# A two-layer attention and MLP kernel on one Trainium2 core: two weight loads moved from ScalarE's queue to GpSimd's, and the order of work settled anew

## The chip, the core and the metric

The kernel runs on one core of one Trainium2 chip. A core has engines that each follow their own list of instructions and wait for one another by semaphores: TensorE (PE; its weight loads are the row PEld), VectorE (DVE), ScalarE (ACT), GpSimd (POOL) and SyncE (SP). SP, ScalarE and GpSimd can issue transfers (DMAs). An engine takes its instructions in order: one that waits holds up all behind it. SBUF is the core's memory of 128 partitions; PSUM, eight banks of 128 x 512 float32, takes TensorE's results. The metric is the device time of one execution, in microseconds (us); less is better.

## The reference

x is 2048 tokens of 512 bfloat16 numbers. Two layers, with the same weights, each do

```python
x = x + A(layernorm(x));  x = x + B(layernorm(x))
# A, linear attention, 32 heads of 16:
q, k, v = split(x @ wqkv);  phi(t) = where(t > 0, t + 1, exp(t)) + 1e-6
kv = phi(k)^T v;  z = sum over tokens of phi(k)        # per head
A  = (phi(q) kv / (phi(q) z + 1e-6)) @ wo
# B: B = gelu(layernorm(x) @ w1 + b1) @ w2 + b2,  512 -> 1792 -> 512
```

## The kernel before

All lies in one function, `build_kernel`. It first makes a graph of operations (each with its engine, its inputs and outputs, and an estimated duration), and then puts them on the engines in an order that is written out: `CONF["ORDER"]` holds one list of names for each engine, and `CONF["WAY"]` says on which engine, or in which form, an operation is done that could be done on several. `Scheduler` walks the lists, gives buffers and PSUM banks in that order, and `assign_waits` turns dependencies into semaphore waits. `N_K`, `N_N` and the like cap how many PSUM banks a class of results may hold while the banks are given out. So the order on the chip is the lists' order, whatever the transfers do.

The tokens are 16 tiles of 128, in four chunks of four. The names used below end in layer and tile, or layer, chunk and part:

- `x0`, `x1`, `xc1`, `xc2`, `xc3`: the loads of x (tile 0, tiles 1 to 3, chunks 1 to 3); `wk`, `wq`, `wv`: the three thirds of wqkv; `wo`; `w1_0`, `w1_1`, `w2_0`, `w2_1`: the halves of w1 and w2, issued by GpSimd through `late` (line 641) after all tiles of layer 0 are turned. x1, xc1, xc2, wq, xc3, wv and wo are issued in this order by ScalarE (lines 613 to 629), x0 and wk by SP.
- `stats`, `aggr` (VectorE), `veps`, `pow` (GpSimd, layer 0's first on VectorE), `norm` (VectorE, or ScalarE with `nmr` on GpSimd ahead): the layer norm of a tile (lines 672 to 697).
- `TA`, `TB`: the turned (transposed) tile, mostly as a DMA of SP (line 707); in the first tiles as `PTA` on TensorE (line 720) with a copy `tcA` by ScalarE (line 730).
- `K`, `Q`: the projections (lines 771, 802, 789); `exp`, `relu` on ScalarE, `min`, `phi` on VectorE or GpSimd: their feature map (lines 741 to 758).
- `G`: products of normed x and phi(k) (line 867, layer 1 line 899), from which `KV` takes the attention state with wv (line 922); `Z`, `zs`, `zb`: the sums z, spread over a mask `bdmask` that GpSimd makes in two steps, `bdm0` and `bdm1` (lines 644 and 647); `M`: the state times wo (line 945).
- `D`, `ln`, `rec`, `pr` (lines 991 to 999): the denominators of a chunk; in other chunks `pz`, `red`, `den`, `rec`, `pr`, `TP` (lines 967 to 983).
- `WO` and `RA` (lines 1015, 1020): the attention's output added to x. `W1`, `gelu`, `W2`, `RB`, `b2` (lines 1047 to 1095, 1032): the MLP. `OD`: the output's store.
- `za`, `zhi`: layer 1's running sum of phi(k). `cpz`, `cpg`, `cpm`: copies out of PSUM. `warm`: ten matmuls on ones, while nothing has been loaded.

The matmul that waits at the start is `K0_0`; it needs `wk` and `tcA0_0`, ScalarE's eighth instruction after seven loads:

```python
"act": "x1 xc1 xc2 wq xc3 wv wo tcA0_0 reluk0_0 tcA0_1 expk0_0 tcA0_2 ..."
```

Of the kernel before, what the change touches and what calls it, by code (L numbers as in the profile page):

```python
# [10 lines left out]
P = 128  # L11
S = 2048
D = 512
# [253 lines left out]
def assign_waits(graph, order, sems, dma_sems):  # L267
# [10 lines left out]
    while len(done) < total:  # L278
        moved = False
        for e in ENGINES:  # L280
# [43 lines left out]
    N_HALF=1, N_K=2, N_Q=3, P_Z0=6.15, N_PB=1, N_PT=8, P_DEN=-50.43, P_A2=-55.11, P_W1=38.59, P_W2=10.23,  # L324
    P_K=55.79, P_G=131.85, P_Q=170.13, STEP=3.86, A1_Q=12.91, A1_STEP=0.5, N_H=4, N_N=3, GAP=28.61,
    ORDER={
        "pe":
            "warm PTA0_0 K0_0 PTA0_1 PTA0_2 K0_1 K0_2 PTA0_4 G0_0_0 PTA0_3 K0_4 K0_3 G0_1_0 Q0_0_0 Q0_0_1 PTA0_5 G0_2_0 K0_5 "
            "K0_7 G0_3_0 Z0_0 K0_6 G0_4_0 K0_8 Q0_1_2 K0_14 G0_5_0 K0_12 Z0_1 K0_15 G0_6_0 Q0_1_3 Q0_1_0 K0_13 G0_7_0 K0_10 "
            "K0_11 Q0_0_2 K0_9 G0_8_0 Q0_1_1 Z0_3 Z0_2 G0_9_0 Q0_0_3 G0_10_0 D0_0_1 G0_11_0 D0_0_0 G0_12_0 D0_0_2 G0_13_0 "  # L330
            "D0_0_3 G0_14_0 D0_1_0 ZR0 G0_15_0 G0_15_1 G0_15_2 Q0_2_0 KV0_0 G0_15_3 KV0_1 D0_1_1 KV0_2 D0_1_2 Q0_2_1 KV0_3 "
            "Q0_2_3 M0_0 M0_2 M0_3 Q0_2_2 M0_1 WO0_0_0 D0_1_3 Q0_3_1 WO0_0_1 WO0_1_0 WO0_0_2 Q0_3_0 WO0_0_3 WO0_3_0 Q0_3_2 "
            "WO0_2_0 WO0_4_0 Q0_3_3 WO0_5_0 WO0_7_0 WO0_6_0 W10_0_3_0 W10_0_4_0 W10_0_0_0 W10_0_9_0 W10_0_1_0 W10_0_7_0 "
            "W10_0_2_0 W10_0_5_0 W10_0_11_0 W10_0_8_0 W10_0_6_0 W10_0_10_0 W10_0_13_0 W20_0_0 W10_0_12_0 W10_0_6_1 W10_0_11_1 "
            "W10_0_0_1 W20_0_7 W10_0_4_1 W10_0_5_1 W10_0_7_1 W20_1_0 W10_0_1_1 W10_0_12_1 W10_0_8_1 W10_0_2_1 WO0_9_0 "
            "W10_0_3_1 W10_0_9_1 W20_1_7 W10_0_10_1 WO0_8_0 W10_1_0_0 W10_1_6_0 W10_1_1_0 W10_1_5_0 W10_1_2_0 W10_1_3_0 "
            "W10_1_4_0 W10_1_13_0 W10_1_12_0 W10_1_10_0 W10_1_7_0 W10_1_8_0 W10_1_11_0 WO0_11_0 WO0_10_0 W20_4_0 W10_1_9_0 "
            "W10_0_13_1 W20_5_0 W20_4_7 W20_5_7 K1_1 W20_7_0 W20_2_0 W20_7_7 W20_6_0 K1_0 W10_2_3_0 W20_6_7 WO0_14_0 "
            "W10_2_0_0 W20_2_7 WO0_13_0 W10_2_10_0 W10_2_1_0 W10_2_12_0 WO0_15_0 W10_2_8_0 WO0_12_0 W10_2_4_0 W10_2_6_0 "
            "W10_2_5_0 W10_2_7_0 W10_2_2_0 W10_2_9_0 W10_2_13_0 W10_2_11_0 W20_8_0 W20_10_0 W20_8_7 W20_10_7 W20_9_0 W20_11_0 "  # L340
            "W20_9_7 W20_3_0 W20_11_7 W10_3_7_0 W10_3_2_0 W10_3_1_0 W20_3_7 K1_2 W10_3_3_0 W10_3_5_0 W10_3_0_0 K1_5 W10_3_6_0 "
            "W10_3_9_0 W10_3_11_0 W10_3_10_0 W10_3_8_0 W10_3_13_0 K1_3 W10_3_12_0 W10_3_4_0 K1_6 K1_4 G1_0_3 G1_0_1 W20_12_0 "
            "G1_0_0 G1_0_2 W20_12_7 K1_7 K1_8 W20_13_0 W20_14_0 W20_13_7 K1_9 W20_14_7 W20_15_0 K1_10 W20_15_7 K1_11 G1_1_0 "
            "G1_1_3 G1_1_1 G1_1_2 Q1_1_1 Q1_1_0 Q1_1_2 K1_13 K1_12 Q1_1_3 Q1_0_0 K1_14 K1_15 Q1_0_2 Q1_0_1 ZH G1_2_1 Q1_0_3 "
            "Z1_3 G1_2_2 G1_3_1 D1_0_0 ZR1 G1_3_2 G1_2_0 G1_3_3 G1_3_0 D1_0_1 G1_2_3 D1_0_2 Q1_3_0 KV1_0 D1_0_3 Q1_2_0 KV1_1 "
            "Q1_3_1 KV1_2 Q1_3_2 KV1_3 Q1_3_3 M1_1 M1_3 M1_2 M1_0 Q1_2_1 WO1_0_0 WO1_1_0 WO1_0_1 Q1_2_2 WO1_0_2 WO1_0_3 "
            "WO1_2_0 WO1_3_0 WO1_4_0 WO1_5_0 PTB1_1 Q1_2_3 PTB1_0 WO1_6_0 W11_0_0_0 W11_0_8_0 W11_0_4_0 W11_0_3_0 W11_0_10_0 "
            "W11_0_12_0 W11_0_5_0 W11_0_2_0 W11_0_13_0 W11_0_1_0 W11_0_6_0 W11_0_9_0 W11_0_7_0 W11_0_11_0 W11_0_1_1 W11_0_2_1 "
            "W11_0_5_1 W11_0_6_1 W11_0_3_1 W11_0_4_1 W11_0_11_1 W11_0_9_1 W11_0_13_1 W11_0_8_1 W11_0_12_1 W11_0_10_1 "
            "W11_0_0_1 W11_0_7_1 WO1_7_0 W21_0_0 W21_1_0 W21_0_7 W21_3_0 W21_1_7 W21_2_0 W21_3_7 W21_2_7 WO1_13_0 W11_1_0_0 "  # L350
            "W11_1_1_0 W11_1_2_0 W11_1_6_0 W11_1_5_0 WO1_12_0 W11_1_10_0 W11_1_13_0 W11_1_3_0 WO1_15_0 W11_1_9_0 W11_1_7_0 "
            "WO1_14_0 W11_1_4_0 WO1_9_0 W11_1_12_0 W11_1_8_0 W21_4_0 W11_1_11_0 WO1_8_0 WO1_10_0 WO1_11_0 W21_5_0 W21_4_7 "
            "W21_6_0 W21_5_7 W21_7_0 W11_3_13_0 W11_3_2_0 W11_3_6_0 W11_3_4_0 W21_7_7 W11_3_0_0 W11_3_1_0 W21_6_7 W11_3_3_0 "
            "W11_3_5_0 W11_3_12_0 W11_2_4_0 W21_12_0 W11_3_10_0 W11_2_1_0 W11_2_5_0 W11_3_8_0 W11_3_7_0 W11_3_11_0 W11_2_12_0 "
            "W11_3_9_0 W11_2_7_0 W11_2_3_0 W11_2_2_0 W11_2_11_0 W11_2_10_0 W11_2_6_0 W11_2_9_0 W11_2_8_0 W11_2_0_0 W21_12_7 "
            "W11_2_13_0 W21_8_0 W21_9_0 W21_8_7 W21_9_7 W21_10_0 W21_13_0 W21_10_7 W21_11_0 W21_13_7 W21_14_0 W21_11_7 "
            "W21_14_7 W21_15_h0 W21_15_h1",
        "act":
            "x1 xc1 xc2 wq xc3 wv wo tcA0_0 reluk0_0 tcA0_1 expk0_0 tcA0_2 reluk0_1 expk0_1 tcA0_4 reluk0_2 tcA0_3 expk0_4 "
            "expk0_2 normA0_7 expk0_3 reluk0_3 expq0_0_0 reluq0_0_0 tcA0_5 expq0_0_1 normA0_8 reluq0_0_1 reluk0_5 normA0_14 "  # L360
            "expk0_5 reluk0_7 expk0_7 expk0_6 normA0_15 normA0_13 reluk0_8 reluk0_14 expk0_8 expk0_14 expk0_12 normA0_10 "
            "expk0_15 normA0_11 expq0_1_3 reluq0_1_3 expq0_1_2 reluk0_13 expq0_1_0 expk0_13 expk0_10 expk0_11 reluk0_11 "
            "expk0_9 expq0_0_2 reluq0_0_2 expq0_1_1 reluq0_1_1 expq0_0_3 ln0_0_1 rec0_0_1 ln0_0_0 rec0_0_0 ln0_0_2 rec0_0_2 "
            "ln0_0_3 rec0_0_3 cpz0 cpg0_2 ln0_1_0 expq0_2_0 rec0_1_0 ln0_1_1 expq0_2_1 rec0_1_1 ln0_1_2 cpm0_0 reluq0_2_1 "
            "cpm0_1 cpm0_3 rec0_1_2 ln0_1_3 rec0_1_3 expq0_2_2 expq0_3_1 reluq0_2_2 expq0_3_0 reluq0_3_0 expq0_2_3 reluq0_2_3 "
            "b1c reluq0_3_1 gelu0_0_4_0 gelu0_0_3_0 gelu0_0_9_0 gelu0_0_1_0 gelu0_0_7_0 gelu0_0_2_0 gelu0_0_0_0 gelu0_0_11_0 "
            "gelu0_0_5_0 gelu0_0_6_0 gelu0_0_8_0 gelu0_0_10_0 gelu0_0_13_0 gelu0_0_12_0 gelu0_0_6_1 gelu0_0_0_1 normB0_6 "
            "gelu0_0_11_1 gelu0_0_7_1 gelu0_0_5_1 gelu0_0_4_1 gelu0_0_1_1 gelu0_0_12_1 gelu0_0_8_1 gelu0_0_2_1 normB0_7 "
            "gelu0_0_9_1 gelu0_0_3_1 expq0_3_2 expq0_3_3 gelu0_0_10_1 gelu0_1_0_0 gelu0_1_6_0 gelu0_1_1_0 gelu0_1_2_0 "
            "gelu0_1_3_0 gelu0_1_4_0 gelu0_1_13_0 gelu0_1_12_0 reluq0_3_3 gelu0_1_10_0 normB0_9 gelu0_1_5_0 normB0_8 "  # L370
            "gelu0_1_7_0 gelu0_1_11_0 gelu0_1_8_0 gelu0_0_13_1 gelu0_1_9_0 normB0_11 expk1_1 gelu0_2_0_0 gelu0_2_3_0 reluk1_0 "
            "gelu0_2_10_0 expk1_0 gelu0_2_12_0 gelu0_2_8_0 gelu0_2_1_0 gelu0_2_4_0 gelu0_2_6_0 gelu0_2_5_0 gelu0_2_2_0 "
            "gelu0_2_7_0 gelu0_2_11_0 gelu0_2_9_0 gelu0_2_13_0 normA1_2 normA1_5 normA1_7 gelu0_3_2_0 gelu0_3_1_0 expk1_2 "
            "gelu0_3_7_0 normA1_6 gelu0_3_5_0 gelu0_3_0_0 gelu0_3_6_0 gelu0_3_9_0 gelu0_3_11_0 reluk1_2 gelu0_3_10_0 "
            "gelu0_3_3_0 gelu0_3_8_0 expk1_5 expk1_3 reluk1_3 gelu0_3_13_0 gelu0_3_4_0 normA1_9 reluk1_6 gelu0_3_12_0 expk1_6 "
            "normA1_11 expk1_4 normA1_10 expk1_7 expk1_8 reluk1_7 reluk1_8 expk1_9 reluk1_9 normA1_12 reluk1_10 expk1_10 "
            "expk1_11 reluk1_11 expq1_1_1 expq1_1_0 normA1_15 reluq1_1_2 expq1_1_2 reluk1_13 expk1_13 expk1_12 expq1_0_0 "
            "reluq1_0_0 expq1_1_3 expk1_14 reluk1_15 expk1_15 expq1_0_2 expq1_0_1 reluq1_1_3 reluq1_0_1 expq1_0_3 reluq1_0_2 "
            "ln1_0_0 cpz1 rec1_0_0 ln1_0_1 rec1_0_1 ln1_0_2 rec1_0_2 reluq1_3_0 expq1_3_0 ln1_0_3 rec1_0_3 reluq1_3_1 "
            "expq1_3_1 cpm1_1 cpm1_3 cpm1_2 expq1_2_0 expq1_3_2 reluq1_3_2 reluq1_2_1 reluq1_2_0 reluq1_3_3 expq1_3_3 "  # L380
            "normB1_1 expq1_2_1 tcB1_1 tcB1_0 gelu1_0_0_0 gelu1_0_4_0 gelu1_0_8_0 gelu1_0_10_0 gelu1_0_3_0 gelu1_0_12_0 "
# [132 lines left out]
def build_kernel(nc, A_x, A_wqkv, A_wo, B_x, B_w1, B_b1, B_w2, B_b2, out, conf=None, report=False):  # L514
# [5 lines left out]
    with ExitStack() as es:  # L520
# [9 lines left out]
        wqkv = SB("wqkv", [P, DT, 3 * D], BF16)  # L530
        wo = SB("wo", [P, DT, D], BF16)
# [108 lines left out]
        def late(name, key, dst, src, prio, kb, after):  # L640
            dma("pool", lambda e: e.dma_start(dst, src), [key], prio=prio, name=name, kb=kb, after=after)
# [635 lines left out]
```

## Time and profile before

| | |
|---|---|
| median of 4 runs | 332.0 us (331.5 to 332.44) |
| the profiled execution | 332.44 us, its span 330.7 us |
| granted TensorE clock, mean | 0.995 |
| TensorE busy | 320.1 us, 97% of the span |
| VectorE, ScalarE, GpSimd busy | 219.1, 199.1, 147.0 us |
| HBM read, written | 8.00 MB, 2.10 MB |

A row of the page's fifth part names line, engine, operation, output and inputs, then how many, busy time and mean length, then the idle time ahead of them and what ended it. "PE ps L771 <- ACT t L730" in a list of waits says that TensorE's instruction of line 771 waited for ScalarE's of line 730. Times within the execution count from the span's start. The granted clock is the share of full speed that TensorE was allowed. An engine name with a small q (ACTq) is its sequencer, as when it issues a DMA.

### The profile page before, as it was taken

The numbers are of one execution on the slowest core, as the hardware profiler recorded it, in microseconds if no ns is written. First come the engines' busy times: TensorE is split into PE (matmuls) and PEld (weight loads), VectorE is DVE, ScalarE is ACT, GpSimd is POOL, SyncE is SP. The second block draws the span as 40 slices with busy tenths as digits, with TensorE's granted clock in tenths as the row PEclk, the third lists the DMA queues.
The fourth block names the chain that finished last, engine by engine and source line by source line (L and its number), as shares of the span: only waits on it lengthen the run. The fifth ranks groups of instructions, "written<-read, shape, count | busy, mean of one in ns | idle before, by whom it ended". The sixth has DMA issues, their size and how long they took to land.

```text
span 330.7 us, 4722 instructions
## 1 busy us (share of the span) xinstructions
PE 320.1 (97%) x1688; PEld 158.7 (48%) x1718; DVE 219.1 (66%) x491; ACT 199.1 (60%) x333; POOL 147.0 (44%) x234
## 2 busy tenths in 40 slices
PE   5999999999999999999999999899999999999996
PEld 1444545486444444444444444448644444444444
DVE  6686677896967667454286889999969777400212
ACT  2697879676981457419992384869944532656200
POOL 3475616659534723336325615657455927000000
PEclk9799999999999999999999999999999999999999
DMA  7833535323112310233010200021143412300011
GB/s 267 257 64 65 135 124 164 92 48 65 33 32 50 63 32 3 48 65 62 2 41 7 52 16 0 2 48 34 33 97 76 84 38 59 80 0 2 16 57 54
DMA packets 49043, 20.37 MB, mean 62 GB/s; under 512 B 41916, under 2 KB 48316, under 8 KB 49020
## 3 DMA queue, kind: packets, MB, share of 16 engines
q1 hardware_dynamic: 44684, 12.86, 17.9%
q0 software_dynamic: 768, 3.67, 3.4%
q10 hardware_dynamic: 3568, 3.54, 3.3%
q8 instruction: 13, 0.21, 0.3%
q14 instruction: 10, 0.08, 0.1%
HBM read 8.00 MB, written 2.10 MB: 31 GB/s over the span
## 4 chain that ended last, share of the span: by engine, by line
PE 84%; DVE 7%; ACT 3%; ACTq 2%; DMA 1%; issue 1%; POOL 0%; DVEq 0%
PE ps L1047 29%; PE ps L1085 28%; PE ps L771 7%; PE ps L1015 7%; PE ps L789 3%; PE ps L867 3%; PE ps L802 2%; PE ps L899 2%; DMA t<-yb 1%; DVE xsb L1020 1%; PE ps L1072 1%; DVE rd L970 1%; ACT eb L741 1%; ACTq L628 1%; DVE rd L973 1%
## 5 line engine op out<-in xcount | busy, mean ns | idle before, releaser
L1053 ACT ACTIVATE gT<-ps,b1c 128x512 bf16<-128x512 f32 (+1 forms) x140 | 78.3, 601 | 65.6 <-PE ps L1047 64.9
L1047 PE MATMUL ps<-t,w 128*128 128x512 bf16 (+1 forms) x556 | 101.5, 336 | 0.3
L1085 PE MATMUL ps<-w,gT 128*128 128x512 bf16 x424 | 96.6, 379 | 0.5
L1047 PEld LDWEIGHTS ps<-t,w 128*128 128x128 bf16 x560 | 54.6, 98 | 44.1 <-ACT t L730 0.3
L1085 PEld LDWEIGHTS ps<-w,gT 128*128 128x128 bf16 x434 | 42.3, 98 | 50.3 <-ACT gT L1053 0.3
L741 ACT ACTIVATE eb<-ps 128x512 bf16<-128x512 f32 x64 | 37.3, 601 | 14.1 <-PE ps L771 7.3
L684 POOL TENSOR_TENSOR rstd<-veps,neghalf 128x1 f32<-128x1 f32 x64 | 37.9, 596 | 6.9 <-DVE veps L682 3.4
L1095 DVE TENSOR_TENSOR outb<-ps,xsb 128x512 bf16<-128x512 f32 x15 | 10.3, 689 | 39.8 <-PE ps L1085 37.8
L771 PE MATMUL ps<-wqkv,t 128*128 128x512 bf16 x125 | 32.3, 388 | 3.5 <-ACT t L730 2.9
L672 DVE BATCH_NORM_STATS2 stats<-xsb 128x6 f32<-128x512 f32 x48 | 32.1, 682 | 0.3
L1015 PE MATMUL ps<-gtb,t 128*128 128x512 bf16 x122 | 30.6, 379 | 0.9 <-DVE xsb L1020 0.3
L752 ACT ACTIVATE rb<-ps 128x512 bf16<-128x512 f32 x43 | 25.1, 606 | 6.1 <-PE ps L771 6.1
L1032 POOL TENSOR_TENSOR xsb<-xsb,b2b 128x512 f32<-128x512 f32 x17 | 20.2, 1195 | 6.1 <-DVE yb L697 6.0
L677 POOL TENSOR_SCALAR veps<-mv 128x1 f32<-128x1 f32 x32 | 8.0, 251 | 32.8 <-DVE mv L674 25.8
L1213 ACT ACT_TABLE_LOAD x17 | 21.8, 1283 | 0.3
L697 DVE TENSOR_SCALAR yb<-xsb,mv,rstd 128x512 bf16<-128x512 f32 x29 | 16.2, 563 | 8.5 <-POOL rstd L684 8.4
L692 ACT ACTIVATE yb<-xsb,nmr,rstd 128x512 bf16<-128x512 f32 x19 | 15.3, 810 | 10.2 <-POOL nmr L689 10.1
L1091 DVE TENSOR_TENSOR xsb<-ps,xsb 128x512 f32<-128x512 f32 x16 | 11.0, 689 | 15.3 <-PE ps L1085 15.2
L771 PEld LDWEIGHTS ps<-wqkv,t 128*128 128x128 bf16 x128 | 12.1, 99 | 18.6 <-ACT t L730 4.2
L789 PE MATMUL ps<-wqkv,t 128*128 128x512 bf16 x78 | 19.9, 379 | 0.1
L754 DVE TENSOR_SCALAR eb<-eb 128x512 bf16<-128x512 bf16 x43 | 14.1, 339 | 8.5 <-ACT eb L741 8.3
L1015 PEld LDWEIGHTS ps<-gtb,t 128*128 128x128 bf16 x128 | 12.2, 98 | 15.5 <-DVE xsb L1020 1.8
(89 smaller groups left out, 381.8 us busy)
## 6 DMA issues: line engine op xcount, KB each, us to landing
w<-in_B_w_dram POOLq DMA_DIRECT2D x4, 896.0 KB, 5.6
out_dram<-outb SPq DMA_DIRECT2D x15, 128.0 KB, 1.7
t<-in_A_x_dram ACTq DMA_DIRECT2D x3, 512.0 KB, 7.2
wqkv<-in_A_wqkv_dram ACTq DMA_DIRECT2D x2, 512.0 KB, 9.2
t<-yb SPq DMA_TRANSPOSE x56, 2.4
wqkv<-in_A_wqkv_dram SPq DMA_DIRECT2D x1, 512.0 KB, 5.2
wo<-in_A_wo_dram ACTq DMA_DIRECT2D x1, 512.0 KB, 9.3
t<-in_A_x_dram ACTq DMA_DIRECT2D x1, 384.0 KB, 3.3
```

The lines of the kernel that those rows point to most:

```text
L672: G.op("dve", lambda e: e.bn_stats(stats[:, s.slot, :], src()), 620, reads=src_keys, writes=[k + "s"], tiles=[s, *src_tiles], prio=prio, n ...
L684: G.op("pool", lambda e: e.tensor_tensor(rstd[:, s.slot:s.slot + 1], veps[:, s.slot:s.slot + 1], neghalf[:], op=ALU.pow), 570, reads=[k + ...
L741: G.op("act", lambda e: e.activation(eb[:, et.slot, :], bank(bt), ACT.Exp), 478, reads=[src_key], writes=[f"e{tag}"], tiles=[bt, et], prio ...
L752: G.op("act", lambda e: e.activation(rb[:, rt.slot, :], bank(bt), ACT.Relu), 478, reads=[src_key], writes=[f"r{tag}"], tiles=[bt, rt], pri ...
L771: ins = e.matmul(bank(b), lhsT=yTa(yT)[:, dt, k * P:(k + 1) * P], rhs=wqkv[:, dt, D:2 * D], start=(dt == 0), stop=(dt == DT - 1))
L789: ins = e.matmul(bank(b), lhsT=yTa(yT)[:, dt, k * P:(k + 1) * P], rhs=wqkv[:, dt, 0:D], start=(dt == 0), stop=(dt == DT - 1))
L1015: ins = e.matmul(bank(wb), lhsT=yTa(pq)[:, kt, k * P:(k + 1) * P], rhs=gtb[:, kt, :], start=(kt == 0), stop=(kt == DT - 1))
L1032: G.op("pool" if on_pool else "dve", lambda e: e.tensor_tensor(xsb[:, st, :], xsb[:, st, :], b2b[:], op=ALU.add), 1120 if on_pool else 600 ...
L1047: ins = e.matmul(bank(b, n), lhsT=w1[:, dt, ft * P:(ft + 1) * P], rhs=yTa(yT)[:, dt, k0 * P:k1 * P], start=(dt == 0), stop=(dt == DT - 1))
L1053: G.op("act", lambda e, ft=ft, b=b, k0=k0, k1=k1, n=n: e.activation(gT[:, g.slot, ft * 512 + k0 * P:ft * 512 + k1 * P], bank(b, n), ACT.Ge ...
L1085: ins = e.matmul(bank(b), lhsT=gT[:, g.slot, ft * 512 + k * P:ft * 512 + (k + 1) * P], rhs=w2[:, ft, :], start=(ft == 0), stop=(ft == FT - 1))
L1213: e.preload_act_table_set(sets[table])
```

## The change

wv and wo are no longer issued by ScalarE. GpSimd issues them through the same helper as w1 and w2, each allowed once tile 5 is turned (`tr` is that turn's last operation). In GpSimd's list wo stands behind nmrA0_13, and wv in a row of five loads.

```diff
-        dma("act", lambda e: e.dma_start(wqkv[:, :, 2 * D:3 * D], wsrc[:, :, 2 * D:3 * D]), ["wv"], prio=-94, name="wv", kb=512)
-        dma("act", lambda e: e.dma_start(wo[:], A_wo.rearrange("(dt p) c -> p dt c", p=P)), ["wo"], prio=-93, name="wo", kb=512)
...
+                if st == 5:
+                    late("wv", "wv", wqkv[:, :, 2 * D:3 * D], wsrc[:, :, 2 * D:3 * D], -88, 512, [tr])
+                    late("wo", "wo", wo[:], A_wo.rearrange("(dt p) c -> p dt c", p=P), -87, 512, [tr])
```

With it all five lists of `ORDER` are new, `N_K` goes from 2 to 4, `N_N` from 3 to 1, and 48 entries of `WAY` change. TensorE's list holds the same operations and differs by neighbours that change places, mostly by one to five us of work. The parts that the prediction speaks of:

```diff
 act:
-x1 xc1 xc2 wq xc3 wv wo tcA0_0 ...
+x1 xc1 wq xc3 xc2 tcA0_0 ...
-... reluq0_0_1 reluk0_5 normA0_14 expk0_5 ...
+... reluq0_0_1 normA0_14 reluk0_7 reluk0_5 ...
 pe:
-... K0_8 Q0_1_2 K0_14 G0_5_0 ...
+... K0_8 K0_14 Q0_1_2 G0_5_0 ...
 pool:
-... nmrA0_13 vepsA0_10 powA0_10 phiq0_0_1 nmrA0_10 ...
+... nmrA0_13 wo vepsA0_10 powA0_10 nmrA0_10 ...
-... powA0_9 phik0_14 bdm1 w2_1 phik0_11 w2_0 phiq0_0_2 pr0_0_3 w1_1 pr0_1_0 pr0_1_1 w1_0 ...
+... powA0_9 phik0_14 w2_0 wv w1_0 w1_1 eps6 w2_1 bdm1 pr0_0_3 pr0_1_0 pr0_1_1 ...
 WAY, from GpSimd to VectorE: b20_4 to b20_7, b20_11, b20_14, b20_15, pz0_3_0, pz0_3_3, pr0_3_2, pr0_3_3,
  phiq0_0_1, phiq0_0_2, phiq0_3_3, phik0_11, phik1_2, phik1_6, phiq1_1_2, za2, za4, za7, ...
 WAY, from VectorE to GpSimd: b20_8, b20_12, pr0_2_3, phiq0_3_0, za5, za11, ...
 WAY, other: normB0_8 from ScalarE to VectorE; phiq1_0_3 from the form with max to relu and add
```

## The prediction

> **What bounds the kernel now.** I read the page first: how full TensorE is, and the chain of work that ended last.
>
> ```profile
> span 330.7 us, 4722 instructions
> ...
> PE 320.1 (97%) x1688; PEld 158.7 (48%) x1718; DVE 219.1 (66%) x491; ACT 199.1 (60%) x333; POOL 147.0 (44%) x234
> ...
> PE 84%; DVE 7%; ACT 3%; ACTq 2%; DMA 1%; issue 1%; POOL 0%; DVEq 0%
> ```
>
> TensorE is the bound nearly everywhere, so only its waits can be won. Then the waits of TensorE, over the whole span (total, times, longest):
>
> ```profile
> PE ps L771 <- ACT t L730: 2.9, 2, 2.5
> ...
> PE ps L771 <- DMA t<-yb: 0.5, 1, 0.5
> PE ps L945 <- DVE kvb L941: 0.5, 1, 0.5
> PE ps L922 <- DVE gtb L912: 0.4, 1, 0.4
> ```
>
> The longest is the first K projection (line 771), which waits for ScalarE's copy of the first turned tile (line 730). Why that copy is late shows in the chain in order of time (start, length):
>
> ```profile
> 3.03 0.59 ACTq L613
> 3.65 2.24 ACTq L628
> 5.92 1.74 ACTq L629
> 7.70 0.61 ACT t L730
> 8.35 1.48 PE ps L771 x4
> ```
>
> ScalarE's sequencer issues seven loads before its first copy. The first five take 0.45 to 0.60 us each, the last two, wv and wo, 2.24 and 1.74: they wait for room, and the copy stands behind them. Last, the table by stretches (PE, PEld, DVE, ACT, POOL busy; granted clock; DMA share; GB/s), cut where the clock changes, and at the seam of the two layers:
>
> ```profile
> 5.40:8.82 3.42, 0.88 (x9) 0.47 (x8) 3.23 (x10) 0.60 (x1) 1.37 (x4) 1.00 1.09 362
> 8.82:12.23 3.41, 3.09 (x14) 1.47 (x13) 1.13 (x6) 2.06 (x4) 2.23 (x6) 0.50 1.11 350
> ...
> 197.00:222.00 25.00, 23.46 (x133) 10.57 (x135) 24.27 (x51) 17.16 (x32) 14.46 (x16) 1.00 0.08 16
> ```
>
> After the stretch in which TensorE mostly stood (0.88 us of 3.42), its clock was 0.50 for 3.41 us. At the seam VectorE is full (24.27 of 25) and TensorE waits.
>
> **The change part by part.** The profiled execution took 332.44 us, 1.74 more than its span; the median is 0.44 below it. I sum against 332.44 and take off 0.44 at the end.
>
> *wv and wo leave ScalarE.* The turn of tile 0 starts at 5.43 on TensorE. Later turns (14.41 and 18.95) have their copies 0.43 us after their start, at 14.84 and 19.38. So tcA0_0 can start at 5.86 instead of 7.70, and K0_0 0.65 behind it (7.70 to 8.35), at 6.51: **-1.84**. What is late next is the K weight itself: issued at 1.25, landing 5.2 us later, 6.45; so no more can be won at this place. All of the chain behind it is fed by K0_0 (reluk0_0, tcA0_1, K0_1, then ScalarE, busy 13.74 us in 12.23 to 27.20). normA0_1 ends at 7.08 and normA0_2 at 8.30, ahead of their turns. xc2 is now issued last, at 3.03; the slowest landing of such a load took 9.0, so it is there at 12.0, and statsA0_8, at 15.01 before, comes to 13.2. Nothing there eats the shift.
>
> *The slow clock.* K0_0 took 1.47 us where four matmuls take 1.03, and the next eight 2.49 where eight take 1.89: 1.04 us of this chain is slow clock. With K0_0 and two turns in it, the stretch before 8.82 would be about 1.9 us busy of 3.42 (0.39 + 1.03 + two turns of 0.25), between the row that was followed by 0.50 (0.88) and the one followed by 1.00 (3.09). Ends 0 and -1.04; I take **-0.4**, as 1.9 is a little nearer to 0.88. The Trainium skill (TensorE: Matmul & The Clock Gate, Part 1) has the clock halved after an idle window of 3.4 us; the row differs, as a window with a quarter of work was followed by half speed. By that rule the whole -1.04 would come, and the sum would be 0.6 lower.
>
> *K0_14 moves ahead of Q0_1_2.* K0_14 waited for the transpose of its tile:
>
> ```profile
> 22.86 4.14 DMA t<-yb
> 27.14 1.02 PE ps L771 x4
> ```
>
> The new order asks for it four matmuls (0.86) sooner, and turns ScalarE's reluk0_5 (0.49 from start to start) behind normA0_14: **+0.37**. Other transposes land in 2.4 at the median; if this one does, the 0.49 of idle time vanishes. Ends -0.5 and +0.9.
>
> *wo's issue on GpSimd* stands ahead of vepsA0_10. The four load issues there took 0.75 to 1.16, so about 0.95; phiq0_0_1 (1.15) leaves the same stretch for VectorE. nmrA0_10 was ready at 27.7 and its user normA0_10 began at 30.42: 2.7 us of cover. Its transfer now runs beside the transposes of tiles 12, 15 and 13. No row of before has a bulk load beside these; 512 KB at the 350 GB/s of the head are 1.5 us, and K0_15, at 30.13, had its transpose issued at 25.51, 2.2 us more than a median landing. Ends 0 and +0.5; I take 0.
>
> The Trainium skill (SBUF - State Buffer, SBUF: two separate sides) speaks against it: a GpSimd load's descriptors are written by that engine, which VectorE's two-port operations lock out, 620 ns becoming 3100 in its example. No row here shows this: the slowest issue took 1.16 with VectorE busy beside it. By the rule wo's issue would be some 2.2 longer, still under the 2.7 of cover, and the sum the same.
>
> *Five loads in a row on GpSimd.* In the new order w2_0, wv, w1_0, w1_1, w2_1 stand ahead of bdm1, the second half of the mask. Before, the mask came first, and issues stood apart:
>
> ```profile
> 33.46 1.25 POOL L758 TENSOR_TENSOR pkb<-eb,rb 128x512 bf16<-128x512 bf16 x1 [3.42 <-DVE eb L754]
> 34.66 0.91 POOL L647 TENSOR_SCALAR_AFFINE_SELECT bdmask<-bdmask 128x512 bf16<-128x512 bf16 x1
> 36.57 1.16 POOL L641 DMA_DIRECT2D w<-in_B_w_dram  x1 [0.99 <-DMA t<-yb]
> 38.47 1.15 POOL L758 TENSOR_TENSOR pkb<-eb,rb 128x512 bf16<-128x512 bf16 x1 [0.74 <-DVE eb L745]
> 39.57 0.95 POOL L641 DMA_DIRECT2D w<-in_B_w_dram  x1
> ```
>
> The first waits for the last transpose, 36.57 before, 34.7 with the shift. Five issues (1.16 + 0.95 + 0.76 + 0.75 + 0.95), eps6 (0.1) and bdm1 (0.91) end at 40.3. zb0, which reads the mask, would be due at 41.91 - 1.84 = 40.07: 0.2 late. It takes 0.69, and D0_0_1 came 1.28 us after its end: covered. Behind the loads wait also eps6 for ln0_0_1 (44.29) and pr0_0_3 (49.44), with room. wv, issued near 36, is read at 50.14 - 1.84 = 48.3, 12 us later, against 7.0 for the longest landing of such a load; wo is read later still. I take 0, the ends are in rival D. Whether GpSimd's queue takes four or five loads at once no row shows; before it had two in flight (issues at 36.57 and 39.57, landing after up to 7.0) and the second cost 0.95. That is rival D.
>
> *Work moved between engines.* In layer 0 five b2 additions (net), two pz, one pr and a norm go to VectorE: 5 x 0.85 + 2 x 0.76 + 0.86 + 0.54 = 7.2 us on top of 56.04 busy in 60 to 135, so 84% of the stretch. The list of TensorE's waits has none between 28 and 197, so this is covered. I take 0; ends 0 and +1.5.
>
> *The seam.* VectorE loses za11 (0.69) and 0.27 by another form of phiq1_0_3, and gains phiq1_1_2 (0.42): -0.5 on the full engine; ScalarE gains a relu (0.60) ahead of cpz1, GpSimd za11 ahead of zhi. I take 0; ends -1.0 and +1.0.
>
> *PSUM caps.* N_K 4 and N_N 1 set which banks the planner may hold; TensorE's order hardly moves and its work is the same (1718 weight loads in both lists). 0.
>
> Sum: 332.44 - 1.84 - 0.4 + 0.37 = 330.57; less 0.44, **330.1**.
>
> **The rivals.**
>
> A, the forecast: ScalarE's head wait is won, the rest cancels: 330.1 (329.2 to 331.3).
>
> B, more: the clock stays full (0.64 more than I took) and K0_14's wait vanishes (0.37 + 0.49): 328.6 (327.6 to 329.2). For it: TensorE has no other wait until the seam. Against: what held the 4.14 us landing the rows do not show, and it may come again.
>
> C, hidden: the shift is given back, 0.9 at K0_14 and 0.9 at the seam, where VectorE is full and starts no sooner than its inputs: 332.0 (331.4 to 332.6). For it: every later wait of TensorE is for the same few producers. Against: these producers hang on K0_0 too, through 170 us of saturated TensorE.
>
> D, slower: GpSimd's queue is full like ScalarE's. That one took 384 + 4 x 512 KB = 2.4 MB and then stopped; here the first three loads are 2.3 MB and the fourth makes it 3.2. If the fourth waits for the first (landing 6.2 after issue, 34.7 + 6.2 = 40.9) and the fifth for the second (some 43), bdm1 ends near 45, zb0 is 4.9 late, and D0_0_1 stands 4.9 - 1.3 = 3.6: 333.7. If only two are held, the third waits until 40.9, the fifth until about 47, and it is 338. It decides once the five issues take 1.1 us longer in all. Against it: issues of 0.75 to 1.16.
>
> E, slower too: at 84% VectorE, a norm in each of four chunks comes 0.7 late: 330.1 + 2.8 = 332.9. Against it: 12 us of VectorE's 75 are still idle there.
>
> That the change does not do what it says, the copy staying late, would need the turn at 5.43 to move; nothing ahead of it changes, so it has no share of its own.
>
> **How the numbers follow.** A 0.43, B 0.17, C 0.13, D 0.18, E 0.09. A difference under 0.2%, 0.66 us, can't be told from none here. Faster (A and B) 0.60, within it (C) 0.13, slower (D and E) 0.27. The range goes from 328.0 into D's first end, 334.0; left out are D's longer end and B's far one, under 0.2.
>
> **What would show it.** ScalarE's first copy at 5.9 and K0_0 at 6.5; ScalarE's five issues done at 3.6. The clock row after 8.8 shows 1.00 or 0.50. K0_14's wait. Five GpSimd issues of about 0.9 each and zb0 near 40. TensorE's waits between 28 and 197 still none. The forecast is wrong if one GpSimd issue takes over 2 us, if zb0 starts after 41.4, or if new waits of TensorE over 1.8 us in all appear.

## The result, and the profile after

The changed kernel takes **329.51 us** in the median of 51 runs (328.57 to 332.55). The kernel before, run again beside it, takes 331.15 us in the median of 77 (329.51 to 333.18); the 332.0 of the four runs above was a little high. The ratio is 0.9951, with a 95% interval of 0.9942 to 0.9961: faster by 1.6 us. The forecast had 330.1, 0.9943 of the time it was given.

The profiled execution took 328.61 us, its span 326.9. It differs from the profiled one of before by 3.8 us, more than the medians do: that one lay 1.3 above its kernel's median, this one 0.9 below its own. So the pair of traces shows where time can go, and only the runs show how often it does. Line numbers after the change are five or so lower: the K projection is line 766, the copy of a turned tile 725, a load by GpSimd 636.

From the page after:

```profile
span 326.9 us, 4727 instructions
...
PE 318.6 (97%) x1687; PEld 159.0 (49%) x1718; DVE 226.9 (69%) x512; ACT 195.4 (60%) x331; POOL 128.8 (39%) x215
...
PE 90%; DVE 6%; DMA 2%; issue 1%; ACT 0%; DVEq 0%
```

ScalarE's sequencer (ACTq) has left the chain. ScalarE's own instructions and issues from the start on show why (start, length):

```profile
0.82 0.45 ACTq L617 DMA_DIRECT2D t<-in_A_x_dram  x1
1.30 0.51 ACTq L610 DMA_DIRECT2D t<-in_A_x_dram  x1
1.83 0.53 ACTq L622 DMA_DIRECT2D wqkv<-in_A_wqkv_dram  x1
2.39 1.30 ACTq L610 DMA_DIRECT2D t<-in_A_x_dram  x2
6.00 0.60 ACT L725 ACTIVATE t<-ps 128x512 bf16<-128x512 bf16 x1 [3.92 <-PE ps L715]
```

Five issues end at 3.69, and the copy now waits for the turn on TensorE, not for the queue: 6.00 in place of 7.70. TensorE's waits after the change, behind the warm-up's 1.5 us, which is the same before and after:

```profile
PE ps L862 <- DVE pkb L742: 0.9, 1, 0.9
PE ps L766 <- ACT t L725: 0.8, 1, 0.8
PE ps L715 <- DVE yb L692: 0.6, 1, 0.6
```

The 2.9 us for the copies fell to 0.8, the 0.5 for a transpose at K0_14 is gone, and two waits are new, which the forecast did not have: 0.9 at G0_9_0 (line 862) for phik0_9, and 0.6 at the turn of tile 2 (line 715) for normA0_2. The same stretches as before, and the seam 2 us earlier (PE, PEld, DVE, ACT, POOL busy; clock; DMA share; GB/s):

```profile
5.40:8.82 3.42, 2.08 (x18) 1.24 (x16) 2.99 (x10) 1.63 (x4) 1.76 (x4) 1.00 1.08 366
8.82:12.23 3.41, 3.41 (x24) 1.65 (x22) 3.38 (x11) 3.10 (x7) 2.83 (x7) 1.00 0.79 247
...
195.00:220.00 25.00, 24.44 (x152) 11.91 (x153) 24.36 (x55) 19.09 (x35) 15.34 (x18) 1.00 0.08 16
```

The clock row stays at 1.00 here, and at the seam TensorE stands for 0.56 of 25 us where it stood for 1.54. How far each operation of TensorE starts ahead of its start in before gives the account of the pair: 1.63 us at K0_0; 2.5 at K0_4, with the clock; 3.16 behind K0_14; 2.3 behind G0_9_0, and so on through 195; 3.7 behind the seam. TensorE's work is the same, so these are its waits and its clock; the wait at tile 2 adds nothing to them, as K0_1 behind it waits until 8.87 for ScalarE's copy anyway.

### The profile page after: what moved, and what is told of

It is laid out like the page before. It is cut to its first block, busy times and chain, and to the rows that moved or that the text cites. A ratio compares the mean times of both kernels' runs of the same rounds, so it can differ in the third digit from the quotient of the medians.

```text
span 326.9 us, 4727 instructions
## 1 busy us (share of the span) xinstructions
PE 318.6 (97%) x1687; PEld 159.0 (49%) x1718; DVE 226.9 (69%) x512; ACT 195.4 (60%) x331; POOL 128.8 (39%) x215
## 3 DMA queue, kind: packets, MB, share of 16 engines
q10 hardware_dynamic: 2512, 2.49, 2.3%
## 4 chain that ended last, share of the span: by engine, by line
PE 90%; DVE 6%; DMA 2%; issue 1%; ACT 0%; DVEq 0%
PE ps L1042 29%; PE ps L1080 29%; PE ps L1010 8%; PE ps L766 8%; PE ps L784 4%; PE ps L862 4%; PE ps L797 3%; PE ps L894 2%; DMA t<-in_A_x_dram 2%; PE ps L1067 1%; DVE gtb L907 1%; DVE rd L965 1%; PE ps L986 1%; PE ps L940 1%; PE ps L843 0%
## 5 line engine op out<-in xcount | busy, mean ns | idle before, releaser
L679 POOL TENSOR_TENSOR rstd<-veps,neghalf 128x1 f32<-128x1 f32 x64 | 39.8, 626 | 7.7 <-DVE veps L677 3.8
L747 ACT ACTIVATE rb<-ps 128x512 bf16<-128x512 f32 x44 | 25.8, 603 | 10.4 <-DVE pkb L753 5.1
L766 PE MATMUL ps<-wqkv,t 128*128 128x512 bf16 x124 | 30.8, 379 | 1.0 <-ACT t L725 0.8
L784 PE MATMUL ps<-wqkv,t 128*128 128x512 bf16 x79 | 19.8, 379 | 0.1
L749 DVE TENSOR_SCALAR eb<-eb 128x512 bf16<-128x512 bf16 x44 | 12.8, 300 | 9.7 <-ACT eb L736 9.7
L687 ACT ACTIVATE yb<-xsb,nmr,rstd 128x512 bf16<-128x512 f32 x18 | 14.5, 812 | 6.6 <-POOL nmr L684 6.6
L1027 POOL TENSOR_TENSOR xsb<-xsb,b2b 128x512 f32<-128x512 f32 x12 | 15.9, 1340 | 4.9 <-ACT yb L687 4.2
```

The lines of the kernel that those rows point to most:

```text
L679: G.op("pool", lambda e: e.tensor_tensor(rstd[:, s.slot:s.slot + 1], veps[:, s.slot:s.slot + 1], neghalf[:], op=ALU.pow), 570, reads=[k + ...
L747: G.op("act", lambda e: e.activation(rb[:, rt.slot, :], bank(bt), ACT.Relu), 478, reads=[src_key], writes=[f"r{tag}"], tiles=[bt, rt], pri ...
L766: ins = e.matmul(bank(b), lhsT=yTa(yT)[:, dt, k * P:(k + 1) * P], rhs=wqkv[:, dt, D:2 * D], start=(dt == 0), stop=(dt == DT - 1))
L784: ins = e.matmul(bank(b), lhsT=yTa(yT)[:, dt, k * P:(k + 1) * P], rhs=wqkv[:, dt, 0:D], start=(dt == 0), stop=(dt == DT - 1))
```

## The experiments

Two theories stood at the outset. **T1**: the gain comes from the two loads leaving ScalarE. **T2**: it comes from the new lists and homes, and the move alone would be given back by later waits. Beside these it was open what the clock is worth, and where the new wait comes from. Ratios are to the kernel before, run beside each.

**The move alone**, the old lists kept:

```diff
 act:  -x1 xc1 xc2 wq xc3 wv wo tcA0_0        +x1 xc1 xc2 wq xc3 tcA0_0
 pool: -nmrA0_13 vepsA0_10 ... bdm1 w2_1      +nmrA0_13 wo vepsA0_10 ... bdm1 wv w2_1
```

> The kernel before with its own lists and homes; only the loads of wv and wo leave ScalarE (wo on GpSimd behind nmrA0_13, wv behind bdm1). T1 (the gain is the move's): K0_0 starts near 6.6 instead of 8.35, and the time is 1.6 to 2.6 us below the kernel before, ratio 0.992 to 0.995. T2 (the gain is that of the new lists; with the old ones later waits give the shift back): K0_0 starts early too, but the ratio is 0.998 to 1.000, and the waits of TensorE after 25 us grow by 1.5 us or more.

> The same kernel as in the first run of the move alone, whose interval (0.9952 to 1.0017) was too wide to decide. T1 (the move brings at least two thirds of the 1.64): ratio 0.994 to 0.997. T2 (the lists bring at least half): 0.998 to 1.000.

Measured: 0.9985 (0.9952 to 1.0017), and in the second round 0.9982 (0.9957 to 1.0007). Both ratios are what T2 expected. K0_0 starts at 6.66 and 6.75, as T1 has it, but in the ratios most of the shift does not reach the end. The two profiles differ. In the first round's (330.24 us) TensorE is 2.17 us ahead of its starts in before from K0_15 to the end of layer 0; nothing is given back. In the second's (332.92 us) the chain of waits shows one place, tile 15's transpose and the K projection that waits for it:

```profile
24.21 5.80 DMA t<-yb
30.01 0.14 issue
30.15 1.02 PE ps L769 x4
```

A transpose takes 2.5 us at the median, this one 5.80; wo's load, issued at 24.52 beside it, took 6.4. TensorE waits 1.83 us for it (line 769), and then the clock follows:

```profile
28.00:31.00 3.00, 1.17 (x17) 0.65 (x15) 1.05 (x3) 1.27 (x2) 1.88 (x5) 1.00 0.92 147
31.00:34.50 3.50, 3.50 (x10) 1.26 (x9) 1.84 (x5) 1.42 (x3) 1.03 (x1) 0.54 0.27 53
```

Against before, TensorE is 1.95 us ahead at K0_12, level at K0_15 and 1.70 behind at K0_13. Of the 24 runs of both rounds 7 have a mean granted clock under 0.997, with a median of 332.79; the other 17 have 330.10.

**The move alone, wo later**: the kernel just told, with wo behind wv instead of behind nmrA0_13.

```diff
 pool: -nmrA0_13 wo vepsA0_10 ... bdm1 wv w2_1   +nmrA0_13 vepsA0_10 ... bdm1 wv wo w2_1
```

> The move alone (old lists) with wo issued behind wv, near 34.5, instead of behind nmrA0_13, near 24. If the move's gain was given back because wo's 512 KB run beside the transposes of tiles 12 and 15 (one took 5.80 us in the profile of the move alone, and TensorE waited 1.83 and then ran 3 us at half clock): tile 15's landing is under 3 us, no run is above 331.5, and the median falls from 330.4 to 329.3 to 329.8, ratio 0.994 to 0.996. If the old lists themselves give it back: the wait ahead of K0_8, K0_12 or K0_15 and the ratio of 0.998 stay.

Measured: 329.43 us (328.03 to 329.66), **0.993** (0.9901 to 0.9958); the interval just touches that of the second round, and the medians of the two rounds (330.34 and 330.52) lie 0.9 and 1.1 us higher. None of its 7 runs has a clock under 0.997. Of the two transposes issued between 23.1 and 24.6 the median landing is now 3.1 us; with wo beside them it was 4.1:

```profile
t<-yb SPq DMA_TRANSPOSE x2, 3.1
```

and, in the second round of the move alone, for 23.1 to 25:

```profile
wo<-in_A_wo_dram POOLq DMA_DIRECT2D x1, 512.0 KB, 6.4
t<-yb SPq DMA_TRANSPOSE x2, 4.1
```

So the old lists can keep the move's gain: with wo later the move alone is worth as much as the whole change, as far as the intervals tell. That this is because wo's 512 KB are out of the transposes' way is shown only for an execution like the second round's. The 3.1 stands between a landing of 2.46 and one of 3.80, so a transpose can be late without wo. And against the first round's profile, which had wo beside the transposes, this one is not ahead at the end of layer 0 (2.00 us ahead of the starts in before, against 2.17); what it has beyond it lies at the seam, where TensorE's waits are 0.3 and 0.2 us instead of 0.5, 0.4 and 0.3. Why these waits come and go with the old lists no run shows.

**The lists alone**: the changed kernel with wv and wo back in ScalarE's list.

```diff
 act:  -x1 xc1 wq xc3 xc2 tcA0_0        +x1 xc1 wq xc3 xc2 wv wo tcA0_0
 pool: -... nmrA0_13 wo ... w2_0 wv w1_0  +... nmrA0_13 ... w2_0 w1_0
```

> The changed kernel with its new lists and homes; only the loads of wv and wo go back to ScalarE, ahead of tcA0_0. T1: tcA0_0 starts at 7.7 again, K0_0 at 8.35 with 0.5 of the clock behind it, and the ratio to the kernel before is 0.998 to 1.002. T2: the ratio stays at 0.995, about what the changed kernel has (0.9951).

> The same kernel as in the first run of the lists alone (0.9988, 0.9965 to 1.0011). T1: 0.999 to 1.000, as the seam's gain of 1.6 in the profile is taken back by the wait of about 1.0 ahead of G0_9_0 and the lost transposes' luck. T2: 0.995 to 0.9975.

Measured: 0.9988 (0.9965 to 1.0011) and 1.0011 (0.9987 to 1.0035): no gain that can be told from none. TensorE's waits at the seam are as short as after the change (0.2 and 0.2 us; 0.5, 0.4, 0.3 and 0.2 before), and the wait of 1.0 to 1.1 at G0_9_0 is there too: the one pays for the other. The changed kernel without the move has lost its whole gain, so T2's first half falls and T1 holds for the new lists. Its second half, that later waits give the move alone back, is what the first two rounds with the old lists showed, and the run with wo later shows that it need not be so.

**The loads on SP**: the changed kernel, with wv and wo in SP's list.

```diff
-late("wv", ...); late("wo", ...)
+dma("sp", lambda e: e.dma_start(wqkv[:, :, 2 * D:3 * D], wsrc[:, :, 2 * D:3 * D]), ["wv"], prio=-94, name="wv", kb=512)
+dma("sp", lambda e: e.dma_start(wo[:], A_wo.rearrange("(dt p) c -> p dt c", p=P)), ["wo"], prio=-93, name="wo", kb=512)
 sp:   -x0 wk b1 b2 TA0_7              +x0 wk b1 b2 wv wo TA0_7
```

> The changed kernel with the loads of wv and wo issued by SP behind b1 and b2, near 6 to 7 us, where SP has nothing else to do until tile 7's transpose. T1 and no cost of GpSimd's issues: 0.9951 as the changed kernel. If the 0.9 us wait ahead of G0_9_0 comes from VectorE's minima being stretched beside five load issues in a row on GpSimd, three of the five are left or four with w2_0 first, and the wait falls to between 0 and 0.6: ratio 0.993 to 0.995. Rival: the two transfers now run beside wq and the last x chunks, which land 1.5 to 3 us later, and some wait of TensorE for them appears between 8 and 20: ratio 0.997 or more.

Measured: 329.85 us, 0.9951 (0.9929 to 0.9973), the changed kernel's own ratio. SP issued them at 10.57 and 11.04 (0.42 and 0.52 us); no wait of TensorE for the x chunks appeared. The wait at G0_9_0 stayed at 1.0 with four loads in a row on GpSimd. Whether GpSimd's or SP's queue carries the two loads matters little; that it is not the one ahead of the first copy matters. Why wv and wo took 2.24 and 1.74 us to issue in ScalarE's queue no run shows; that it had no room left is inferred from the five issues before them.

**The filled stretch**, what the clock is worth in the kernel before:

```diff
+def fill(e):
+    for _ in range(10):
+        ins = e.matmul(bank(wu, D), lhsT=onesm[:, 0:P], rhs=onesm[:, 0:D], start=True, stop=True)
+    return ins
 pe:   -warm PTA0_0 K0_0               +warm PTA0_0 fill K0_0
```

> The kernel before with ten idle matmuls of 512 columns between PTA0_0 and K0_0, where TensorE waits for ScalarE's copy anyway; nothing else. If the slow clock after the idle stretch is what costs: the stretch 5.4 to 8.8 is over 2.5 of 3.42 busy, the next one has clock 1.00, K0_0 takes 0.86 to 1.03 instead of 1.47 and the time falls by 0.6 to 1.0 us, ratio 0.997 to 0.998. Rival: the chain behind K0_0 hangs on ScalarE and VectorE and gives the faster matmuls back: ratio 0.9995 to 1.0005 at clock 1.00. Slower than 1.001 if the idle matmuls run at half speed themselves and end after 8.35.

Measured: 331.14 us, 0.9989 (0.997 to 1.0007). The idle matmuls kept the clock:

```profile
8.06 1.04 PE L777 MATMUL ps<-wqkv,t 128*128 128x512 bf16 x4 [0.31 <-ACT t L736]
...
10.27 2.02 PE L777 MATMUL ps<-wqkv,t 128*128 128x512 bf16 x8 [0.73 <-ACT t L736]
```

K0_0 took 1.04 instead of 1.47 and the next eight 2.02 instead of 2.49, but between them TensorE waits 0.73 for ScalarE's copy, where it waited 0.32. None of its 12 runs has a mean granted clock under 0.997; of 83 runs of the kernel before taken beside the experiments 47 have, with a median of 331.23 against 331.45 for the rest. The interval reaches from a gain of 1.0 us to a loss of 0.2, so the runs do not decide. The medians speak for the rival, that the slow stretch at the head hides behind ScalarE; but they go by the granted clock, which can read full while matmuls are slow (last section). The profile speaks against it: TensorE is ahead of its starts in before by 0.29 us at K0_0, whose copy came at 7.41 instead of 7.70, by 1.20 at K0_4, and by 1.27 at the end of layer 0. So ScalarE's copies take back some 0.4 us there, and 0.9 gets through. What the clock costs in the old order stays open between the two. In the changed kernel 7 runs have such a clock, with a median of 330.95, and the others 329.34.

**The new wait**, from two sides. First the loads late: on GpSimd bdm1 ahead of them, wv behind it, and the four loads of w1 and w2 held until G0_9_0 is done.

```diff
+g9 = [o for o in G.ops if o.name == "G0_9_0"]
-late(f"w1_{h}", ..., trs); late(f"w2_{h}", ..., trs)
+late(f"w1_{h}", ..., trs + g9); late(f"w2_{h}", ..., trs + g9)
 pool: -phik0_14 w2_0 wv w1_0 w1_1 eps6 w2_1 bdm1   +phik0_14 bdm1 wv eps6 w1_0 w1_1 w2_0 w2_1
```

> The changed kernel with bdm1 ahead of the loads on GpSimd, wv right behind it, and the four loads of w1 and w2 only once G0_9_0 is done. If the GpSimd issues stretch VectorE's minima (0.70, 0.95 and 0.75 us beside them against 0.29), the minima of tiles 11 and 9 are back at 0.29, phik0_9 comes 0.9 to 1.1 earlier, the wait ahead of G0_9_0 is under 0.2, and the time falls by 0.6 to 0.9 below the changed kernel's: ratio to the kernel before 0.992 to 0.994. If VectorE's new order alone makes tile 9 late, the minima shrink or not, but the wait stays at 0.5 or more and the ratio at 0.995. Slower than the changed kernel if the weights of the first MLP matmuls, now issued near 39 to 42, land after their use near 60.

Measured: **328.12 us** (327.47 to 328.9), 0.9903 (0.9882 to 0.9923). GpSimd and VectorE after the change; the minima are lines 740 and 749:

```profile
33.43 1.03 POOL L636 DMA_DIRECT2D w<-in_B_w_dram  x1 [0.93 <-DMA t<-yb]
34.45 0.78 POOL L636 DMA_DIRECT2D wqkv<-in_A_wqkv_dram  x1
35.23 1.46 POOL L636 DMA_DIRECT2D w<-in_B_w_dram  x2
...
36.72 0.96 POOL L636 DMA_DIRECT2D w<-in_B_w_dram  x1
```

```profile
33.84 0.70 DVE L740 TENSOR_SCALAR eb<-eb 128x512 bf16<-128x512 bf16 x1 [0.46 <-ACT eb L736]
...
35.52 0.95 DVE L749 TENSOR_SCALAR eb<-eb 128x512 bf16<-128x512 bf16 x1
...
36.85 0.29 DVE L749 TENSOR_SCALAR eb<-eb 128x512 bf16<-128x512 bf16 x1
37.05 0.75 DVE L740 TENSOR_SCALAR eb<-eb 128x512 bf16<-128x512 bf16 x1
37.84 0.69 DVE L742 SCALAR_TENSOR_TENSOR pkb<-ps,eb 128x512 bf16<-128x512 f32 x1
```

and VectorE with the loads late:

```profile
34.04 0.35 DVE L740 TENSOR_SCALAR eb<-eb 128x512 bf16<-128x512 bf16 x1 [0.38 <-ACT eb L736]
...
35.37 0.28 DVE L749 TENSOR_SCALAR eb<-eb 128x512 bf16<-128x512 bf16 x1
...
36.69 0.29 DVE L740 TENSOR_SCALAR eb<-eb 128x512 bf16<-128x512 bf16 x1 [0.37 <-ACT eb L736]
37.02 0.69 DVE L742 SCALAR_TENSOR_TENSOR pkb<-ps,eb 128x512 bf16<-128x512 f32 x1
```

These are the same minima, of tiles 10, 11 and 9; the row of 36.85 is another one's, minq0_0_2. Of the three long ones, all beside issues, two ended 0.08 and 0.12 us after an issue did (34.54 after 34.46, 37.80 after 37.68). Not every minimum beside an issue is long: that of 36.85 began 0.13 us into one and took 0.29, and in the kernel before two began 0.13 and 0.02 us into one (36.70 and 39.59) and took 0.28 and 0.29. The three long ones began 0.29 to 0.41 us into one. With the loads later they are back at 0.28 to 0.35, phik0_9 starts at 37.02 instead of 37.84, and the wait at G0_9_0 is gone. w1 and w2, issued at 39.26 to 42.57, are in time: TensorE waits for neither. The wait explains 0.9 of the 1.4 us in the medians; what the rest comes from is not shown.

Then from TensorE's side, Q0_0_3 put into the wait, with the loads as the change has them:

```diff
 pe:   -Z0_3 G0_9_0 Z0_2 Q0_0_3 G0_10_0   +Z0_3 Q0_0_3 G0_9_0 Z0_2 G0_10_0
```

> The changed kernel with one move on TensorE: Q0_0_3 (four matmuls, 0.86) ahead of G0_9_0 instead of behind Z0_2, so that it fills the wait for phik0_9. If the 0.86 wait is on the path that sets the end: the wait is under 0.2 and the time 0.6 to 0.9 below the changed kernel's, ratio 0.992 to 0.994. If it is given back (the chunk sums, dz0 and D0_0_1 behind it, or the seam): the waits move to D0_0_1 or to 195 to 212 and the ratio stays at 0.995.

Measured: 328.59 us (328.33 to 329.15), 0.9919 (0.9899 to 0.9938). That is 0.9 below the changed kernel, the first case. The minima stay long (0.71, 0.95, 0.75), but TensorE has other work meanwhile. A part is given back, at D0_0_1:

```profile
PE ps L986 <- DVE zb L923: 0.4, 1, 0.4
```

Both together, with no further edit:

> The late loads (bdm1 and wv first, w1 and w2 once G0_9_0 is done, wo where the change put it) together with Q0_0_3 ahead of G0_9_0. If both edits remove one and the same wait: within 0.3 us of the late loads alone (328.1, ratio 0.990), not lower by another 0.9. If they remove different losses: 327.3 or less. Worse than the late loads if w1 and w2, which now wait 0.86 longer for G0_9_0, or the wait of 0.53 ahead of D0_0_1 come back: 328.6.

Measured: 328.66 us, 0.9931 (0.9908 to 0.9955). No second gain: the two edits remove one and the same wait. The 0.4 ahead of D0_0_1 is there again, and the time is that of the expectation's last case; that it is worse than the late loads alone is not shown, as the intervals overlap.

**Two attempts at more**, both on top of the late loads. wo behind wv (`pool: ... bdm1 wv wo eps6 w1_0 ...`):

> The kernel with the late loads (bdm1 and wv first, w1 and w2 once G0_9_0 is done), and wo moved from behind nmrA0_13, near 24 us, where it runs beside the transposes of tiles 15, 13 and 10, to behind wv, near 34.5. If wo's transfer costs something beside the transposes in the new order: the waits of 0.3 ahead of K0_8 to K0_15 and the upper end of the runs go, 0.2 to 0.5 us less than the 328.1 of the late loads. If not: 328.1 within 0.3. More than 328.5 if wo's issue at 34.3 to 35.2 stretches VectorE's minima of tiles 10 and 11 again.

Measured: 328.44 us, 0.9924 (0.9893 to 0.9956), no gain. In the new order wo's issue, at 23.89 after the change, stands a microsecond behind those of tiles 12 and 15 (21.54 and 22.85), which land in 2.5 us; tile 13's, behind it, took 4.1 and was in time. With the old lists wo came 0.3 to 0.4 behind a transpose that TensorE was about to need (22.48 behind 22.08, 24.52 behind 24.21). And, besides, three idle matmuls each in the two waits of the head (`pe: warm PTA0_0 fill0 K0_0 PTA0_1 fill1 PTA0_2`):

> The late loads with wo behind wv and, besides, three idle matmuls each in the two waits of the head, ahead of K0_0 and of PTA0_2. If the clock still falls in some runs because of these waits: no run shows a clock under 0.997, and the median is 0.1 to 0.3 below the kernel without them. If not: equal within 0.2. Slower by up to 0.8 if the first three run at half clock and end after the copy that K0_0 waits for.

Measured: 328.98 us, 0.9932 (0.9907 to 0.9958), no gain either. The late loads alone are the fastest version run, 1.4 us below the changed kernel in the medians, with an interval (up to 0.9923) that ends below the changed kernel's (from 0.9942).

## Why the prediction was right

*wv and wo leave ScalarE, -1.84*: right in kind, 0.2 too large. K0_0 came at 6.72, not 6.51: the turn of tile 0 took 0.53 us instead of 0.39, so the copy started at 6.00 instead of 5.86. The K weight landed at 6.59, the next bound as said. One reading was wrong: normA0_2, at 8.30 in before, was not ahead of its turn, which was due at 7.98; TensorE waits 0.57 for it, at no cost, as told above. That the lists alone bring nothing, and the loads on SP as much as those on GpSimd, makes the move the source of the gain.

*The slow clock, -0.4*: in the pair of traces 0.92 (K0_0 1.47 to 1.02, the next eight 2.49 to 2.02, which is the whole term less 0.1), and 0.9 in the profile of the filled stretch; over the runs that gives 0.36 by its ratio, within a wide interval. The size taken was a middle between a full and a halved clock, and that it is near 0.36 is luck. The idle stretch is not all that decides, either: in the two profiles of the move alone, one kernel, TensorE waited 0.88 and 0.69 ahead of K0_0, and K0_0 took 1.02 and 1.89.

*K0_14, +0.37*: the sign was wrong. Its transpose landed in 2.65 us instead of 4.14, and there was no wait: -0.65 in the pair, beyond the end of -0.5. The 4.14 was a landing of one execution, and the forecast was built on it, though it said that the rows do not show what held it.

*wo's issue, 0*: right in the changed order. That its transfer may hurt the transposes was said and priced at up to 0.5; with the old lists it seems to cost 0.9 to 1.7 us (medians, and 0.998 against 0.993), though part of that may be the seam's. In the one execution where its path is seen, the delay of a transpose beside it and the slow clock behind that cost 3.65 us (from 1.95 ahead to 1.70 behind), far beyond the upper end; the forecast had no term for the clock there.

*Five loads in a row, 0*: wrong by 0.86 us. The issues took 0.73 to 1.03 each, as said, and rival D, the full queue, did not come: bdm1 ended at 38.6, earlier than forecast. What was missed is what GpSimd's issues can do to VectorE beside them. The Trainium skill (SBUF — State Buffer, SBUF: two separate sides) calls the port pair of the two engines an exclusive lock that whoever starts first holds for its whole instruction. The forecast weighed only the half in which VectorE holds up GpSimd; the runs show VectorE held up, with three minima at 0.70 to 0.95 beside issues and 0.28 to 0.35 when these are later. That it is this lock, and not another thing that the two share, the runs do not separate, and the minimum that began inside an issue and still took 0.29 differs from the page's whole instruction.

*VectorE from 60 to 135, 0*: right: 59.64 us busy there, 80%, and no wait of TensorE. Rival E did not come.

*The seam, 0 with ends of 1.0*: the pair's lead grew there from 2.3 to 3.7, so 1.4 beyond the value taken and 0.4 beyond the end. In all nine profiles with the new lists TensorE's waits at the seam come to 0.4 us; in the five with the old ones to 0.3, 0.5, 1.0, 1.2 and 1.4. So with the new lists they are short in every profile, with the old ones only in some; the three operations counted did not price it.

In the pair the terms come to 3.7 (1.6, 0.9, 0.65 and 1.4 won, 0.86 lost), in the medians to 1.64, so the runs do not price each term, and that the sum came within 0.6 us is in part luck: K0_14 and the seam were better, G0_9_0 worse. What decided the forecast, the wait at the head and its size, was right, and the experiments carry it.

## What to carry to other kernels

When loads in the queue of an engine that also computes stand ahead of its first use and wait there, try another queue; here GpSimd's and SP's did equally well. Ask then what their transfer runs beside. GpSimd's load issues were not always free for VectorE: look at them where VectorE is late in a chain, and give TensorE other work there. Before pricing a wait by one profiled execution, ask whether it is a landing, or a clock, that varies.

## What the runs showed of the hardware

A matmul can run at near half speed while the granted clock in the rows says 1.00. In one profile of the lists alone K0_0 took 1.89 us for four matmuls and the next eight 3.29, where the changed kernel's took 1.02 and 2.02, while the rows of the stretches say this:

```profile
5.40:8.82 3.42, 1.32 (x8) 0.69 (x7) 3.06 (x10) 0.60 (x1) 1.81 (x4) 1.00 1.07 362
8.82:12.23 3.41, 3.09 (x14) 1.52 (x13) 1.00 (x5) 2.06 (x4) 2.24 (x6) 1.00 1.10 348
```

Full speed came near 14 us in that execution, in the changed kernel's profile before 6.7. The two profiles of the move alone, the same kernel, show it too: K0_0 at 1.02 and 1.89, both in rows of 1.00. So here the duration of a known matmul tells the clock better than the row does. The Trainium skill (TensorE: Matmul & The Clock Gate, Part 1) says that the window which decides runs free and that the number of slow matmuls at the start differs from run to run; these two profiles agree with the second, and no run here shows the first.
